# First-stage steps in other gaps and, for two batches, in whole passes, in a Fourier-mixing kernel with a fused feed-forward layer

## The chip, the cores and the metric

One core of one Trainium2 chip. The metric is the device time of one execution in microseconds (us), as the median of three runs. The engines are TensorE (PE, with its weight loads shown as PEld), VectorE (DVE), ScalarE (ACT), GpSimd (POOL) and SyncE (SP). ACT, POOL and SP also issue DMAs; each engine works through its own instructions in program order. All times below are us unless marked otherwise; in the profile's groups the mean of one instruction is in ns.

## What is computed

Eight batches of 3008 tokens with 256 channels are filtered in the frequency domain along the tokens, and the result goes through a feed-forward layer whose nonlinearity is h - tanh(h):

```python
X = np.fft.rfft(x, axis=1)                       # x: (8, 3008, 256)
Y = X * (filt_r + 1j * filt_i)[None]             # 1505 frequencies, 256 channels
y = np.fft.irfft(Y, n=3008, axis=1).reshape(-1, 256)
h = y @ w_in                                     # (24064, 256) @ (256, 2048)
out = (h - np.tanh(h)) @ w_out                   # (24064, 2048) @ (2048, 256)
```

## The kernel before, in words

**The stages.** The transform of 3008 = 64 x 47 points is done as matrix products. For one batch there are four stages:

- *first* (L245 to L280): the transform over the 64, for residues r and 47 - r at once. A step takes four residues: `x_sb` holds token rows of r in partitions 0 to 63 and those of 47 - r in 64 to 127, `f` the matrices. For each pair of PSUM banks it runs eight 64x64 products (quarters of the array); fp32 makes two passes of each, so the trace shows sixteen. ACT copies the second bank to `other` (L271), DVE writes sum and difference to `a1` (L272, L273), and two DMAs bring a1 to DRAM (`ct1`). Those are put on the list `written` and issued by ACT at the next gap (L1256). A batch has six such steps. Batch 0 and the first eight residues of batch 1 are done in a prologue instead, with whole 128-column passes (`first0`, `first1`).
- *middle* (L370 to L402): for seven slots of frequencies, products pa and pb (`forth`), the filter on DVE (`filtered`, L331 to L352), and the way back pe0 and pe1 (`back`, L362 to L367). It is a generator, with 58 steps that each issue one piece.
- *last* (L460): the product pu for 4 residues of tokens, ACT's copy `odd` (L475), DVE's sums into `ut` (L478, L479).
- the *feed-forward layer*: for each group of four residues (six groups c to a batch, 48 groups i) four units u, so U = 4i + u runs from 0 to 191. `up` (L499) multiplies by w_in into banks x, y, z (L512) with a Strassen-like scheme of seven products; ACT and DVE evacuate them (L518, L535, L552, L560, L568); `shrink` computes h - tanh(h) of the unit before with three ACT passes (L624, L627, L630) and a DVE product (L634); `down` multiplies the unit before that by w_out into o (L682). The first four units use the plain scheme (`up_plain`, L582, and `down_plain`, L736).

**The order.** It is written out by hand; the program order is each engine's order. In `up` five gaps t(0) to t(4) are left, in which other stages may issue. For batches 1 and up PE's order in a unit is

`x1 y2 | t(0) | o | t(1) | x6 z5 o | t(2) | x7 o x4 | t(3) | o | t(4) | z3`

Line L535, which reads bank y, is issued on DVE after t(0) and o. In t(k) (L1252) at most one planned step is issued, *last* always at u = 3, k = 2. The planner (`planned`) gives each step a due position on the scale pos = 20c + 5u + k; while batch p's tokens are computed it spreads six first-stage steps of batch p + 2 over 0.2 to 104, and the 58 middle steps of batch p + 1 likewise (for p = 0: ten first-stage steps, batch 1's last four and batch 2's six, from 4 to 34, and the middle steps from 34). A gap takes the first of the two next steps that is due and allowed.

**The banks.** Two PSUM banks, t and y, serve these stages. y is also unit U's own. A first-stage step and *last* take both (`zd2`), a middle product takes one (`zd`): y if a dictionary `taken`, kept by gap, says that t was given to another shortly before, else t. `taken` is cleared when a middle product comes in gap 0, and only then.

**The tiles.** `tr` has a1 with one buffer and e1 with two. Tag e1 is used for `other`, `odd`, the `e1` of `back`, and the a1 of `first1`'s last two steps (residues 4 to 7 of batch 1), whose stores SP issues (L1070).

**The end of the prologue** (L1126 to L1145). `rest` issues on SP the four loads of `e2` for slots 0 to 4 (L967), `way_back` then runs the last slot's `back`, whose stores go to ACT and SP (L367), and `rest` loads the other slots. Then come the first loads of `first(2, ...)` on SP (L253, L232, L238), the conversion of the float64 weights (`converted`: ACT L158, DVE L160, L163, L166, L169, L171, L178, one step at each `next`), first1's last stores and four steps of the remaining conversions. The conversions go on in the gaps of U = 0 to 5.

Of the kernel before, what the change touches and what calls it, by code (L numbers as in the profile page):

```python
# [9 lines left out]
F32 = mybir.dt.float32  # L10
# [15 lines left out]
XH = 4  # L26
# [22 lines left out]
def _consts():  # L49
    q = np.arange(NQ)[:, None]  # L50
    k1 = np.arange(1, NA)[None, :]

    def angle(r):
        return 2 * np.pi * ((k1 * (NR * q + r)) % SEQ) / SEQ

    def sign(r):
        return (-1.0) ** ((q[:, 0] + r) % 2)

    f = np.zeros((2, NQ, NH, 2, NA))
    g = np.zeros((4, NA, NH, 2, NQ))  # L60
    for r in range(NH):
        for half, n in ((0, r), (1, NR - r)):
            if half and not r:
                continue
            odd = 1.0 - 2 * half
            c, s = np.cos(angle(n)), np.sin(angle(n))
            plus, minus = (1 + sign(n)) / 2, (1 - sign(n)) / 2
            f[half, :, r, 0, :-1], f[half, :, r, 1, :-1] = c, -odd * s
            f[half, :, r, 0, -1], f[half, :, r, 1, -1] = plus, minus
            g[0, :-1, r, half], g[1, :-1, r, half] = 2 * c.T, -2 * s.T  # L70
            g[2, :-1, r, half], g[3, :-1, r, half] = -2 * odd * s.T, 2 * odd * c.T
            g[0, -1, r, half], g[2, -1, r, half] = plus, minus
            g[1, -1, r, half], g[3, -1, r, half] = odd * minus, odd * plus
    g = g[BLOCKS, :] / SEQ

    t = 2 * np.pi * (np.outer(np.arange(NH), np.arange(NH)) % NR) / NR
    cos, sin = np.cos(t), np.sin(t)
    twice = np.where(np.arange(NH) > 0, 2.0, 1.0)[:, None]
    mats = np.zeros((KM, 6 * KM + 8 * KH))
    for k, m in enumerate((cos, sin, -sin)):  # L80
        way = np.einsum("rm,st->srmt", m, np.eye(SG))
        mats[:, k * KM:k * KM + KM] = way.reshape(KM, KM)
        mats[:, (3 + k) * KM:(4 + k) * KM] = way.reshape(KM, KM).T
    for k, (a, b) in enumerate(((cos, cos), (cos, -sin), (sin, cos), (-sin, -sin),
                                (cos, twice * cos), (cos, -2 * sin),
                                (sin, twice * cos), (-sin, -2 * sin))):
# [5 lines left out]
    return [np.ascontiguousarray(v, dtype=np.float32)  # L92
            for v in (f.reshape(128, -1), g[:, :, :, 0].reshape(128, -1), g.reshape(128, -1),
                      mats, np.eye(128))]

@with_exitstack
def kernel(
# [8 lines left out]
):  # L106
    nc = tc.nc
    V, G, ACT = nc.vector, nc.gpsimd, nc.scalar
    f_d, g_d, whole_d, mats_d, one_d = (
        nc.inline_tensor(v, name=n).ap()  # L110
        for v, n in zip(_consts(), ("f", "g", "g_whole", "mats", "one")))

    ct1 = [nc.dram_tensor(f"ct1_{b}", (4 * NA * NH, DM), F32, kind="Internal")
           for b in range(1, BATCH)]
# [130 lines left out]
    def first(b, z, also=()):  # L245

        jobs = [*also, *((b, c) for c in range(NX))]

        def begin(k):
            b, c = jobs[k]  # L250
            w = XH * 64
            f = tr.tile([128, XH, 64], F32, tag="f", bufs=2, name="f")
            nc.sync.dma_start(f, f_d[:, w * c:w * (c + 1)])  # L253
            return load_x(tr.tile([128, XH, DM], F32, tag="x", bufs=2, name="x_sb"),
                          b, XH * c, XH), f

        began = [begin(0), begin(1)]
        yield
        for k, (b, c) in enumerate(jobs):
            xt, f = began.pop(0)  # L260
            banks = z("pf", [128, 2, DM])
            for n in range(2):
                for bank, half in zip(banks, rows):
                    for m, out_half in enumerate(rows):
                        nc.tensor.matmul(bank[out_half, n], f[half, 2 * m + n], xt[half, 2 * m + n],  # L265
                                         start=True, stop=True)
            if k + 2 < len(jobs):
                began.append(begin(k + 2))
            a1 = tr.tile([128, 2, 2, DM], F32, tag="a1", bufs=1, name="a1")
            other = tr.tile([128, 2, DM], F32, tag="e1", bufs=2, name="other")  # L270
            ACT.copy(other, banks[1])  # L271
            V.tensor_add(a1[:, 0], banks[0], other)  # L272
            V.tensor_sub(a1[:, 1], banks[0], other)  # L273
# [609 lines left out]
    with tc.tile_pool(name="tr", bufs=2) as tr, tc.manual_schedule():  # L883
# [12 lines left out]
        with tc.tile_pool(name="pro", bufs=1) as pro, \  # L896
# [163 lines left out]
            def first1(x1):  # L1060

                for r in range(0, 8, 2):
                    pf = z0("pf", [128, 2, DM])
                    for k in range(2):
                        nc.tensor.matmul(pf[:, k], f0[:, r + k], x1[:, r + k],
                                         start=True, stop=True)
                    a1 = (pro.tile([128, 2, DM], F32, tag="e1", bufs=4, name="a1") if r < 4 else
                          tr.tile([128, 2, DM], F32, tag="e1", bufs=2, name="a1"))
                    ACT.copy(a1, pf)
                    (ACT if r < 4 else nc.sync).dma_start(  # L1070
                        dram(ct1[1], r * DM, [[NH * DM, 128], [1, 2 * DM]]), a1)
                    yield
# [23 lines left out]
            for g in range(last_g + 1):  # L1096
                if g + 2 <= last_g:
                    fts[g + 2] = filters_of(g + 2)
                    a2[g + 2] = across(g + 2)
                if g == 3:  # L1100
                    e2s[0] = load_e2(0, 0, ())
                    ones_1 = first1(load_x(big([128, 8, DM], F32, "x1"), 1, 0, 8))
                if g == last_g - 1:
                    under(fts[last_g])
                    convert(3)
                    way_back()
                if g < last_g:
# [12 lines left out]
                if g not in (0, last_g - 1):  # L1120
                    way_back()
                if g == 1:
                    next(turning)
                if g == 2:
                    ahead = [begun(tiles1, job, queue=G) for job in jobs[5:7]]
            rest(0, SG * (last_g - 1), [nc.sync])  # L1126
            way_back()
            rest(SG * (last_g - 1), NA - SG * (last_g - 1), [nc.sync])
            fs = first(2, z2, [(1, c) for c in range(2, NX)])
            next(fs)  # L1130
# [3 lines left out]
            next(late)  # L1134
            for _ in ones_1:
                pass
            for _ in range(4):
                next(late)
            warmer(10)

        with tc.tile_pool(name="dn", bufs=2) as dn, \
# [4 lines left out]
            def zd(name, shape):  # L1146
                U, k = now
                if U < 4:
                    tag = taken["plain"] = "ty"[taken.get("plain") == "t"]
                    return ps.tile(shape, F32, tag=tag, bufs=1, name=name)  # L1150
                if k == 0:
                    taken.clear()
                tag = "y" if (k == 1 and taken.get(0) == "pb" or
                              k == 2 and taken.get(1) not in (None, "y") or
                              k == 3 and taken.get(2) != "y") else "t"
                taken[k] = "y" if tag == "y" else name
                return ps.tile(shape, F32, tag=tag, bufs=1, name=name)

            def zd2(name, shape):
# [47 lines left out]
            for U in range(total + 2):  # L1207
# [44 lines left out]
                def t(k):  # L1252

                    now[:] = U, k
                    while written:
                        ACT.dma_start(*written.pop(0))  # L1256
                    if k == 2 and stores:
# [77 lines left out]
```

## Time and profile before

| what | us |
|---|---|
| three runs | 2705.08, 2706.46, 2701.56 |
| median | 2705.08 |
| the profiled execution | 2712.48 |
| its span | 2710.6 |
| prologue, up to the first tokens' product in x (L582) | 0 to 96.5 |
| first-stage steps, first and last (L265) | 104.9, 1997.1 |

The profile is that of a single execution, which was itself a little longer than the runs. A row of the timeline gives the start in us from the span's start, the length, the engine, the line, the operation, out<-in, the count of merged instructions, and in brackets the idle time before it with what ended it. Matmuls overlap: a pass of 256 columns is shown at about 0.38, though the next one starts 0.216 behind it. A row of waits gives who waited for whom, the total, how often, and the longest. In the groups by line there follow busy time, mean of one in ns, and the idle time before, with its causes.

### The profile page before, as it was taken

The numbers are of one execution on the slowest core, as the hardware profiler recorded it, in microseconds if no ns is written. First come the engines' busy times: TensorE is split into PE (matmuls) and PEld (weight loads), VectorE is DVE, ScalarE is ACT, GpSimd is POOL, SyncE is SP. The second block draws the span as 40 slices with busy tenths as digits, with TensorE's granted clock in tenths as the row PEclk, the third lists the DMA queues.
The fourth block names the chain that finished last, engine by engine and source line by source line (L and its number), as shares of the span: only waits on it lengthen the run. The fifth ranks groups of instructions, "written<-read, shape, count | busy, mean of one in ns | idle before, by whom it ended". The sixth has DMA issues, their size and how long they took to land.

```text
span 2710.6 us, 41489 instructions
## 1 busy us (share of the span) xinstructions
PE 2644.6 (98%) x15540; PEld 2287.9 (84%) x15540; DVE 1805.7 (67%) x2254; ACT 1678.9 (62%) x2507; POOL 1303.8 (48%) x1084
## 2 busy tenths in 40 slices
PE   8889999999999999999999999999999999999998
PEld 6458888888898888988889888898888988898887
DVE  6787766676666666667656776577765776655555
ACT  3455666656666666666666666666666666666665
POOL 4115555454455444644445444455444554555552
PEclk9899999999999999999999999999999999999999
DMA  8754332331324313332234222332322222111110
GB/s 213 208 141 97 87 70 65 81 91 46 70 70 106 73 33 73 91 88 67 47 70 107 64 67 51 82 88 65 78 56 57 47 62 50 28 26 28 21 23 18
DMA packets 331881, 196.91 MB, mean 73 GB/s; under 512 B 225215, under 2 KB 302635, under 8 KB 331607
## 3 DMA queue, kind: packets, MB, share of 16 engines
q1 hardware_dynamic: 289357, 135.90, 21.6%
q10 hardware_dynamic: 38138, 45.63, 6.0%
q0 software_dynamic: 4176, 12.64, 1.7%
q8 instruction: 124, 2.03, 0.3%
q14 instruction: 86, 0.70, 0.1%
HBM read 121.91 MB, written 75.00 MB: 73 GB/s over the span
## 4 chain that ended last, share of the span: by engine, by line
PE 90%; DVE 5%; DMA 2%; issue 1%; ACT 1%; POOL 0%; SPq 0%; ACTq 0%; DVEq 0%; POOLq 0%
PE o L682 39%; PE x L512 23%; PE z L512 11%; PE y L512 5%; PE pe L362 3%; PE pu L471 2%; PE pa L314 2%; PE pf L265 1%; PE pb L314 1%; DVE h L634 1%; DVE xy L352 0%; DMA x<-in_x_dram 0%; DMA ct<-a 0%; DVE xy L351 0%; DMA mats_sb<-mats 0%
## 5 line engine op out<-in xcount | busy, mean ns | idle before, releaser
L682 PE MATMUL o<-t,wd 128*128 128x256 f32 (+1 forms) x3008 | 762.5, 376 | 0.0
L634 DVE TENSOR_TENSOR h<-h,y 128x1024 f32<-128x1024 f32 (+1 forms) x384 | 555.9, 1448 | 189.1 <-ACT y L630 188.6
L492 POOL TENSOR_TENSOR t<-h 128x512 f32<-128x512 f32 (+1 forms) x186 | 249.2, 1340 | 841.1 <-DVE h L634 782.2
L682 PEld LDWEIGHTS o<-t,wd 128*128 128x128 f32 x3008 | 572.0, 191 | 69.8 <-issue 3.9
L512 PE MATMUL x<-tu,wu 128*128 128x256 f32 (+1 forms) x2256 | 580.0, 380 | 4.4 <-ACT u L518 4.3
L682 PE MATMUL o<-h,wd 128*128 128x256 f32 (+1 forms) x2256 | 570.7, 376 | 1.8 <-DVE h L634 1.8
L512 PEld LDWEIGHTS x<-tu,wu 128*128 128x128 f32 x2256 | 421.3, 190 | 66.8 <-ACT u L518 10.5
L682 PEld LDWEIGHTS o<-h,wd 128*128 128x128 f32 x2256 | 428.7, 190 | 52.0 <-DVE h L634 2.6
L518 ACT COPY s<-x 128x512 f32<-128x512 f32 (+1 forms) x188 | 108.6, 578 | 532.9 <-PE x L512 527.1
L624 ACT ACTIVATE y<-h 128x1024 f32<-128x1024 f32 (+1 forms) x384 | 400.2, 1042 | 27.4 <-ACT e L365 8.0
L627 ACT ACTIVATE y<-y 128x1024 f32<-128x1024 f32 (+1 forms) x384 | 399.3, 1040 | 12.1
L630 ACT ACTIVATE y<-y 128x1024 f32<-128x1024 f32 (+1 forms) x384 | 399.9, 1041 | 4.7
L495 POOL TENSOR_TENSOR t<-h,t 128x512 f32<-128x512 f32 (+1 forms) x186 | 275.3, 1480 | 0.0
L518 ACT COPY u<-x 128x512 f32<-128x512 f32 (+1 forms) x376 | 214.6, 571 | 88.8 <-PE x L512 79.7
L493 POOL TENSOR_TENSOR t<-h,t 128x512 f32<-128x512 f32 (+1 forms) x186 | 261.0, 1403 | 14.6
L494 POOL TENSOR_TENSOR t<-h 128x512 f32<-128x512 f32 (+1 forms) x186 | 260.1, 1398 | 0.0
L560 DVE COPY h<-x 128x512 f32<-128x512 f32 (+1 forms) x188 | 127.8, 680 | 141.9 <-PE x L512 141.3
L512 PE MATMUL x<-ut,wu 128*128 128x256 f32 (+1 forms) x752 | 191.3, 377 | 4.1 <-DVE h L560 4.0
L512 PE MATMUL y<-ut,wu 128*128 128x256 f32 (+1 forms) x752 | 191.0, 377 | 0.0
L512 PE MATMUL z<-tu,wu 128*128 128x256 f32 (+1 forms) x752 | 191.0, 376 | 0.0
L552 DVE TENSOR_TENSOR h<-z,u 128x512 f32<-128x512 f32 (+1 forms) x188 | 126.7, 674 | 96.3 <-ACT u L518 95.0
L512 PE MATMUL z<-ut,wu 128*128 128x256 f32 (+1 forms) x752 | 190.8, 376 | 0.0
(160 smaller groups left out, 2965.3 us busy)
## 6 DMA issues: line engine op xcount, KB each, us to landing
e<-ct SPq DMA_DIRECT2D x47, 512.0 KB
ct<-a ACTq DMA_DIRECT2D x82, 256.0 KB
ct<-e ACTq DMA_DIRECT2D x86, 240.0 KB
a<-ct SPq DMA_DIRECT2D x42, 480.0 KB
ft<-filt SPq DMA_DIRECT2D x42, 480.0 KB
out_dram<-ot SPq DMA_DIRECT2D x1248, 16.0 KB
x_sb<-in_x_dram SPq DMA_DIRECT2D x74, 256.0 KB
gt<-g SPq DMA_DIRECT2D x48, 128.0 KB
```

The costliest lines, as they stand in the source:

```text
L492: by.tensor_sub(t[0], b[0][1], b[0][0])
L493: by.tensor_sub(t[1], b[1][1], t[0])
L494: by.tensor_sub(t[2], b[1][1], b[0][1])
L495: by.tensor_sub(t[3], b[1][0], t[1])
L512: nc.tensor.matmul(bank[:, k], wu[:, q - 1, (2 * u + k) * 128:(2 * u + k + 1) * 128], rhs[q - 1], start=(first and k == 0), stop=True, ski ...
L518: ACT.copy(t, X)
L560: V.tensor_copy(h[:, 2, :, 0:w], X)
L624: ACT.activation(y[k], ht[k], AF.Arctan, scale=TURN)
L627: ACT.activation(y[k], y[k], AF.Tanh, scale=BEND)
L630: ACT.activation(y[k], y[k], AF.Square, scale=SCALE, accum_out=y_sums[:, 2 * U + k // 2:2 * U + k // 2 + 1])
L634: V.tensor_mul(ht[k], ht[k], y[k])
L682: nc.tensor.matmul(product(q), wd[:, q - 1, (2 * u + k) * 128: (2 * u + k + 1) * 128], rhs[q - 1][:, k], start=(u == 0 and k == 0 and q == ...
```

## The change

1. `first` for batches up to 2 (ten steps): a matrix `f` of 128 columns from a new constant `both`, so that one whole pass gives both signs; four products (eight passes) in place of eight quarters, two ACT copies straight into a1, no `other` and no DVE sums, and one DMA from ACT right behind the copies. The tile `f` and its load grow from 128 to 256 KB for these steps.
2. `taken` is cleared at gap 0 of every unit from U = 4 on, and keeps the gap of the last "pb".
3. From U = 4 on a first-stage step may go only into gaps 1 and 2 of units 0 to 2, and not into the gap behind a "pb". Before, all gaps but 0 were allowed.
4. `first1`'s last two a1 are halves of one tile of tag a1, no longer e1.
5. `way_back` stands ahead of the first `rest`.
6. The four conversion steps at the prologue's end go; the same steps are then the first that come after the first tokens' *last*.

```diff
+    both = np.concatenate([f, np.stack([f[0], -f[1]])], axis=3)
...
         def begin(k):
             b, c = jobs[k]
-            w = XH * 64
-            f = tr.tile([128, XH, 64], F32, tag="f", bufs=2, name="f")
-            nc.sync.dma_start(f, f_d[:, w * c:w * (c + 1)])
+            n = 64 if b > 2 else 128
+            f = tr.tile([128, XH, 128], F32, tag="f", bufs=2, name="f")[:, :, 0:n]
+            w = XH * n
+            nc.sync.dma_start(f, (f_d if b > 2 else both_d)[:, w * c:w * (c + 1)])
...
             banks = z("pf", [128, 2, DM])
+            a1 = tr.tile([128, 2, 2, DM], F32, tag="a1", bufs=1, name="a1")
+            if b <= 2:
+                for m, bank in enumerate(banks):
+                    for n in range(2):
+                        nc.tensor.matmul(bank[:, n], f[:, 2 * m + n], xt[:, 2 * m + n],
+                                         start=True, stop=True)
+                    ACT.copy(a1[:, m], bank)
+                if k + 2 < len(jobs):
+                    began.append(begin(k + 2))
+                ACT.dma_start(dram(ct1[b], XH * c * DM, [[NH * DM, 128], [1, XH * DM]]),
+                              a1.rearrange("p m n c -> p (m n c)"))
+                yield
+                continue
...
-            a1 = tr.tile([128, 2, 2, DM], F32, tag="a1", bufs=1, name="a1")
...
+                    if r == 4:
+                        two = tr.tile([128, 2, 2, DM], F32, tag="a1", bufs=1, name="a1")
                     a1 = (pro.tile([128, 2, DM], F32, tag="e1", bufs=4, name="a1") if r < 4 else
-                          tr.tile([128, 2, DM], F32, tag="e1", bufs=2, name="a1"))
+                          two[:, r // 2 - 2])
...
+            way_back()
             rest(0, SG * (last_g - 1), [nc.sync])
-            way_back()
             rest(SG * (last_g - 1), NA - SG * (last_g - 1), [nc.sync])
...
-            for _ in range(4):
-                next(late)
             warmer(10)
...
-                if k == 0:
-                    taken.clear()
...
+                if name == "pb":
+                    taken["slow"] = k
...
                     now[:] = U, k
+                    if k == 0 and U >= 4:
+                        taken.clear()
...
                         due = [s for s in steps[0:2] if s[0] <= pos and
-                               (k or U < 4 or s[3] is middle)]
+                               (s[3] is middle or U < 4 or
+                                u < 3 and 0 < k < 3 and taken.get("slow") != k - 1)]
```

More of the change, by code (lines that the diff above doesn't have):

```diff
@@ L92, in _consts @@
     return [np.ascontiguousarray(v, dtype=np.float32)
-            for v in (f.reshape(128, -1), g[:, :, :, 0].reshape(128, -1), g.reshape(128, -1),
-                      mats, np.eye(128))]
+            for v in (f.reshape(128, -1), both.reshape(128, -1), g[:, :, :, 0].reshape(128, -1),
+                      g.reshape(128, -1), mats, np.eye(128))]
 @with_exitstack
@@ L108 @@
     V, G, ACT = nc.vector, nc.gpsimd, nc.scalar
-    f_d, g_d, whole_d, mats_d, one_d = (
+    f_d, both_d, g_d, whole_d, mats_d, one_d = (
         nc.inline_tensor(v, name=n).ap()
-        for v, n in zip(_consts(), ("f", "g", "g_whole", "mats", "one")))
+        for v, n in zip(_consts(), ("f", "f_both", "g", "g_whole", "mats", "one")))
     ct1 = [nc.dram_tensor(f"ct1_{b}", (4 * NA * NH, DM), F32, kind="Internal")
```

## The prediction, as it stood before the run

> **What bounds the kernel now.** I read the page's busy shares and its chain first, then the busy time by stretches, then PE's waits, and last the timeline at each wait.
>
> ```profile
> span 2710.6 us, 41489 instructions
> PE 2644.6 (98%) x15540; PEld 2287.9 (84%) x15540; DVE 1805.7 (67%) x2254; ACT 1678.9 (62%) x2507; POOL 1303.8 (48%) x1084
> PE 90%; DVE 5%; DMA 2%; issue 1%; ACT 1%; POOL 0%; SPq 0%; ACTq 0%; DVEq 0%; POOLq 0%
> ```
>
> PE is busy for nearly the whole span and holds 90% of the chain. The page's share is a mean over two different stages, so I asked for them apart (start and end, then busy time of PE, PEld, DVE, ACT, POOL, granted clock, DMA share, GB/s):
>
> ```profile
> 97.00:202.00 105.00, 94.88 (x470) 54.54 (x470) 88.30 (x161) 56.76 (x89) 11.93 (x13) 0.95 0.59 166
> 440.00:767.00 327.00, 323.14 (x1936) 282.35 (x1936) 220.06 (x267) 207.05 (x309) 163.38 (x132) 1.00 0.30 73
> ```
>
> From 97 to 202 us (units U = 0 to 6: batch 0's tokens while the weights are converted) PE is idle for a tenth and DVE, with conversions, is nearly as full. From 440 us on, each batch takes 327 us, and PE lacks only 3.9 of them. There PE is the limit: a pass more or a wait more costs its own length. So the waits decide (us in total, times, longest):
>
> ```profile
> PE pf L265 <- DVE xy L320: 7.6, 5, 1.5
> PE x L582 <- DVE ut L479: 6.2, 1, 6.2
> PE pe L362 <- DVE a L273: 5.4, 5, 1.1
> PE pa L314 <- issue: 5.2, 5, 1.0
> PE pe L362 <- DVE h L535: 1.2, 6, 0.2
> ```
>
> Four of the five come five times or six: once in each of the batches in which a batch's first stage (3 to 7) runs beside the tokens. The 6.2 is the start of the first tokens.
>
> **The change, part by part.**
>
> *The gaps of the quarter steps.* I worked through the planner's list: due times of a first-stage step 17.3 apart, those of the 58 middle steps 1.79 apart, one step to a gap, the gap of the tokens' own first product left out. As (token group c, unit u, gap k), the six steps of each of batches 3 to 7 lie now at (0,0,1), (0,3,4), (1,3,1), (2,2,3), (3,2,1), (4,1,3). By the new rule they lie at (0,0,1), (1,0,1), (2,0,1), (3,0,1), (3,2,2), (4,2,1).
>
> What goes: at (3,2,1) a step takes both banks one gap after "pb" took t; and after (2,2,3) and (4,1,3) a middle product wants t one gap behind. The timelines of PE and DVE show the first, a step without a wait (535.05), and one of the latter (start, length, instruction):
>
> ```profile
> 535.05 1.10 PE L265 MATMUL pf<-x_sb,f 64*64 64x256 f32 x16
> 536.08 1.13 PE L512 MATMUL x<-tu,wu 128*128 128x256 f32 x4
> ...
> 633.33 1.67 PE L682 MATMUL o<-h,wd 128*128 128x256 f32 x7
> 636.53 1.59 PE L265 MATMUL pf<-x_sb,f 64*64 64x256 f32 x16 [1.53 <-DVE xy L320]
> 638.05 1.13 PE L512 MATMUL x<-tu,wu 128*128 128x256 f32 x4
> ...
> 686.44 1.13 PE L682 MATMUL o<-t,wd 128*128 128x256 f32 x4
> 688.65 1.09 PE L362 MATMUL pe<-xy,mats_sb 120*120 120x256 f32 x4 [1.08 <-DVE a L273]
> ```
>
> and the chain gives the spacing of whole passes, eight in 1.73, 0.216 each:
>
> ```profile
> 207.93 1.73 PE o L682 x8
> ```
>
> A step without a wait holds PE for 536.08 - 535.05 = 1.03. At (3,2,1) seven passes from 633.33 end at 634.84, and X goes on at 638.05: 3.21, of which 1.03 is the step and some 0.1 the change of shape, so 2.1 is waiting. After (4,1,3), four passes from 686.44 end at 687.30 and pe starts at 688.65: 1.35. The wait of pa after (2,2,3) is as long by the waits (5.2 beside 5.4 for five): 1.3. In group 5, pe waits for L535 because a stale record put it into bank y; the record is now cleared at each unit's gap 0, so it goes to t: 0.2 to 0.4, say 0.3. Together 2.1 + 1.35 + 1.3 + 0.3 = 5.05 a batch, **25.2 for five**.
>
> What comes: the rule knows of "pb", but not of a late read of bank y, which L535 does on DVE. At (1,0,1), (3,0,1) and (4,2,1) the gap before holds a pe, a pe and a product on SBUF, with L535 in time; (3,2,2) comes two gaps after pb. At (2,0,1), however, gap 0 gives DVE L351 and L352 ahead of L535. That unit before, where no first-stage step follows:
>
> ```profile
> 546.11 1.03 PE L512 MATMUL z<-ut,wu 128*128 128x256 f32 x4
> 548.70 1.89 PE L682 MATMUL o<-h,wd 128*128 128x256 f32 x8
> 550.43 1.03 PE L512 MATMUL x<-tu,wu 128*128 128x256 f32 x4
> ...
> 545.80 1.21 DVE L349 TENSOR_TENSOR nn<-nn,xy 120x512 f32<-120x512 f32 x1
> 546.93 1.21 DVE L634 TENSOR_TENSOR h<-h,y 128x1024 f32<-128x1024 f32 x1
> 548.07 0.68 DVE L568 TENSOR_TENSOR h<-z,u 128x512 f32<-128x512 f32 x1
> 548.67 1.45 DVE L351 TENSOR_TENSOR xy<-nn 120x512 f32<-120x512 f32 x1
> 550.04 1.76 DVE L352 TENSOR_TENSOR xy<-nn 120x512 f32<-120x512 f32 x1
> 551.73 0.68 DVE L535 TENSOR_TENSOR h<-y,s 128x512 f32<-128x512 f32 x1
> ```
>
> The step would start at 550.43 and want y after its first four quarter passes, at about 550.85. L535 ends at 552.41: a wait of 1.55. But L349 moves two gaps earlier with its "sub", and L272/L273 of the old (1,3,1) leave the unit before, so L568 need not wait for L634: z's passes from 546.11 are done about 547.1, up to 0.9 earlier than 548.07. So the wait is 0.7 to 1.55; I take 1.1, **5.5 for five**. Queued behind it on PE is everything (X's passes, the next o products), so it counts in full. Net of the gaps: **-19.7** (bounds -17.5 and -21.7 by that wait).
>
> *Whole passes for batches 1 and 2* (ten steps, U = 0 to 6; only U = 5's second moves, to U = 6's gap 2). PE: eight passes of 0.216 = 1.73 for 1.03 and two changes of shape of some 0.1, so +0.5 to +0.7 a step, **+6**. The Trainium skill (TensorEngine Tiling (Array Packing), Available Configurations) has four independent 64x64 tiles; by it sixteen quarter passes would last as long as four whole ones, 0.86, and the edit would cost 0.87 a step, 8.7 in all. The rows have the quarters dearer than that, and they decide.
>
> What DVE and ACT lose and get (busy us, mean ns, idle time before):
>
> ```profile
> L272 DVE TENSOR_TENSOR a<-pf,other 128x512 f32<-128x512 f32 x10 | 6.9, 688 | 7.5 <-DMA ct<-a 4.1 <-ACT other L271 2.7 <-ACT conv L158 0.6
> L273 DVE TENSOR_TENSOR a<-pf,other 128x512 f32<-128x512 f32 x10 | 6.8, 680 | 0.0
> L160 DVE TENSOR_SCALAR conv<-conv 128x512 f32<-128x512 f32 x10 | 4.6, 465 | 4.4 <-ACT conv L158 4.4
> L163 DVE TENSOR_SCALAR conv<-conv 128x512 int32<-128x512 int32 x10 | 4.5, 453 | 0.3
> L166 DVE SCALAR_TENSOR_TENSOR conv<-raw,conv 128x512 int32<-128x512 int32 x10 | 6.9, 690 | 0.3
> L271 ACT COPY other<-pf 128x512 f32<-128x512 f32 x10 | 5.8, 579 | 7.5 <-PE pf L265 7.5
> L1256 ACTq DMA_DIRECT2D ct<-a x20: 582/619/686, 108.0 to 195.9; - x20
> ```
>
> DVE loses 13.7 of adds, and its 7.5 of waits ahead of them pass to ACT. ACT gets a second copy (+5.8) and loses ten of twenty DMA issues (-6.2): even. SP loads f with 256 instead of 128 KB, ten times. The four conversion steps taken out of the prologue are ACT's scaling and L160, L163, L166: 0.47 + 0.45 + 0.69 = 1.6 of DVE work that lay in idle time and now falls behind the first tokens' sums. The new hold: a1 has one buffer, so ACT's copy of the next step waits for the last one's DMA, with the activations, the h and u copies and the conversions' scaling queued behind it; hardest at U = 6, gaps 1 and 2, some 5 apart. Ends for the stage: all of DVE's relief counts, -13.7 - 4.1 + 1.6 = -16; none of it counts, +6. PE, 94.88 of 105 busy, has 10 to give and takes 6 more, so the middle of what is left, **-6**.
>
> *The first tokens.* ACT, SP and PE at their start:
>
> ```profile
> 87.98 2.40 PE L471 MATMUL pu<-gt,e 64*64 64x64 f32 x64 [3.60 <-DMA e<-ct]
> 96.55 3.36 PE L582 MATMUL x<-ut,wu 128*128 128x448 f32 x4 [6.17 <-DVE ut L479]
> 94.72 0.58 ACT L475 COPY odd<-pu 128x512 f32<-128x512 f32 x1 [8.51 <-DMA ct<-a]
> 89.57 1.02 SPq L1070 DMA_DIRECT2D ct<-a  x2
> ```
>
> pu is done at 90.4, but its copy "odd" starts at 94.72: its e1 buffer is that of first1's third a1, whose store SP issues only at 89.57, behind the loads. With a1 in a buffer of its own, odd can start at about 90.5: **-4.2**. Late next is nothing but pu, and pu waits for e<-ct. way_back before rest puts two stores ahead of four loads on SP; the last loads wait for those stores either way: 0, at most +1.5 if the four land later.
>
> **Sum**: -19.7 - 6 - 4.2 = -29.9. The profiled execution took 2712.48 (its span and 1.9 around it), so it would take 2682.6; it lies 7.4 above the median of the runs, 2705.08, and off that the forecast is **2675.2**.
>
> **Rivals.**
>
> 1. *The wait on y is longer and comes at more gaps.* For it: L351 and L352 above take 1.45 and 1.76, and L349, of the same 120x512, took 1.21; a DVE that falls behind by one such excess at (1,0,1), (3,0,1) and (2,0,1) makes waits of about 0.5, 0.5 and 2. The batches then save 25.2 - 15 = 10: 2685. Against it: pe, not a DVE sum, stands in gap 0 of two of them. The Trainium skill (GPSIMD Engine Reference, Specifications) has POOL share SBUF interfaces with DVE, in contention with instructions of two SBUF inputs; L351 and L352 are such, and POOL's combination would start earlier there, so by it the wait grows rather than shrinks; the rows of 1.21 and 1.76 agree.
> 2. *The early stage gives nothing:* PE's +6 is paid and DVE's relief ends in waits for the raw weights or for a1. -19.7 - 4.2 + 6 = -17.9: 2687. For it: the DMA share of 0.59 and ACT's 4.4 ahead of L160.
> 3. *L535 is always in time and DVE was the early limit:* -25.2 - 4.2 - 12 = -41: 2664.
> 4. *Slower: ACT held by a1's single buffer.* With the hold h at each of the ten early steps passed on to PE, 6 + 10h stands against 23.9 saved; it decides from h = 1.8 on. At the 4.1 of the one such wait above it is 6 + 41 - 23.9 = +23: 2728. Against it: of ten such waits nine didn't occur, with steps mostly 5 to 15 apart.
> 5. *The rule doesn't reach what it means:* the steps meet as long a wait in the new gaps (25 against 25), and the early stage pays what the start saves: 2705.
>
> **How the numbers follow.** Forecast 0.50 (2666 to 2684), rival 1 0.17, rival 2 0.15, rival 3 0.12, rival 4 0.04, rival 5 0.02. The range takes in the forecast and rivals 1 and 2 with some 4 for the runs' own spread, and the half of rival 3 that lies nearer: 2663 to 2691. A measurement of this kernel tells about 0.2%, 5.4 us. All but rivals 4 and 5 are faster by more: 0.94; the same 0.02; slower 0.04.
>
> **What would show it.** Right: no wait of pf on L320, none of pe on L273 or pa; a wait of pf on L535, five times about 1; a batch of about 323.4 in place of 327.3; "odd" right behind pu, U = 0 at about 92.4; L272 and L273 thirty times instead of forty; U = 7 some 10 earlier than at 202. Wrong: ACT's copies of a1 waiting for ct<-a for several us in U = 1 to 6, PE's x waiting for ACT there, or a batch still at 327.

## The result, and the profile after

| | before | after |
|---|---|---|
| median | 2705.50 | 2680.40 |
| runs | 2701.56 to 2706.46 (4) | 2680.11 to 2681.72 (4) |
| span of the profiled execution | 2710.6 | 2678.3 |

The ratio is 0.9911, with a 95% interval of 0.9894 to 0.9928: 25.1 us faster, beside 29.9 forecast. The medians put the time at 2680.4, 5.2 above the point of the forecast and inside its range. The two profiles differ by 32.3, since the profiled execution of before lay above its median. One execution of before in a later series of runs took 2794.03 at a granted clock of 0.945 and is left out of the medians and ratios below.

In the changed kernel the lines have moved: the quarters' product L265 is now L280 and the adds L272 and L273 are L286 and L287; the whole passes have L268, their copies to a1 L270 and their DMA L273; L312 to L402 and what follows stand 14 further down (L512 is L526, L535 is L549, L362 is L376, L475 is L489, L582 is L596, L736 is L750). The head of the page after:

```profile
span 2678.3 us, 41269 instructions
PE 2641.6 (99%) x15460; PEld 2292.6 (86%) x15460; DVE 1780.1 (66%) x2234; ACT 1684.2 (63%) x2517; POOL 1312.4 (49%) x1084
PE 91%; DMA 3%; DVE 2%; issue 1%; ACT 1%; SPq 1%; POOL 0%; ACTq 0%; DVEq 0%; POOLq 0%
```

PE has 80 instructions fewer and nearly the same busy time, 2641.6 for 2644.6: the gain is idle time, not work. The busy time by stretches of after, for U = 0 to 6 and for one later batch (columns as before):

```profile
92.00:193.00 101.00, 97.76 (x391) 64.82 (x392) 78.41 (x145) 62.95 (x100) 12.14 (x13) 0.95 0.63 193
428.00:752.00 324.00, 322.64 (x1935) 281.98 (x1935) 218.88 (x267) 207.02 (x309) 163.43 (x132) 1.00 0.31 74
```

In the batch PE now lacks 1.4 of 324 where it lacked 3.9 of 327. In the early stretch PE lacks 3.2 of 101 (it lacked 10.1 of 105), with DVE's load 10 lower and ACT's 6 higher. PE's waits after, over the whole span (some rows left out):

```profile
PE pu L485 <- DMA x_sb<-in_x_dram: 4.9, 1, 4.9
PE x L526 <- ACT u L532: 4.6, 6, 0.9
PE o L750 <- DVE wd L179: 3.2, 1, 3.2
PE x L596 <- DVE ut L493: 1.9, 1, 1.9
PE pf L280 <- DVE h L549: 1.4, 5, 0.5
```

The three waits that came five times in before (7.6 of pf for xy, 5.4 of pe, 5.2 of pa) are gone. Three stand in their place: five of pf for L549, as forecast; x for ACT's u, five of them in the later batches (before has 4.3 of these in four waits, all ahead of the batches); and a single one of 3.2 for the weights. The last two the forecast did not have. The lengths of stretches, read from the timelines (start of the first x product of a unit to that of the next; each batch's 24 units from U = 24):

| | before | after |
|---|---|---|
| start of U = 0 | 96.5 | 91.9 |
| U = 0 to 6 | 105.2 | 100.5 |
| of these, U = 2 | 18.3 | 15.5 |
| of these, U = 3 | 17.9 | 23.2 |
| of these, U = 4 | 18.4 | 14.3 |
| of these, U = 5 and 6 | 34.0 | 30.3 |
| U = 7 to 23 | 238.8 | 234.9 |
| of these, U = 9 | 18.1 | 14.1 |
| five batches with first-stage steps | 327.3 327.3 327.3 329.0 327.6 | 324.4 324.1 324.5 324.3 324.1 |
| the batch without them | 315.3 | 314.8 |

### The profile page after: what moved, and what is told of

The parts are those of the page before. It is cut to its first block, busy times and chain, and to the rows that moved or that the text cites. A ratio compares the mean times of both kernels' runs of the same rounds, so it can differ in the third digit from the quotient of the medians.

```text
span 2678.3 us, 41269 instructions
## 1 busy us (share of the span) xinstructions
PE 2641.6 (99%) x15460; PEld 2292.6 (86%) x15460; DVE 1780.1 (66%) x2234; ACT 1684.2 (63%) x2517; POOL 1312.4 (49%) x1084
## 3 DMA queue, kind: packets, MB, share of 16 engines
q8 instruction: 123, 2.02, 0.3%
## 4 chain that ended last, share of the span: by engine, by line
PE 91%; DMA 3%; DVE 2%; issue 1%; ACT 1%; SPq 1%; POOL 0%; ACTq 0%; DVEq 0%; POOLq 0%
PE o L696 40%; PE x L526 24%; PE z L526 12%; PE y L526 6%; PE pe L376 3%; PE pu L485 2%; PE pb L328 2%; PE pa L328 1%; PE pf L280 1%; PE o L750 1%; DMA out_dram<-ot 1%; DMA filt<-in_filt_r_dram 1%; SPq L802 0%; PE pf L268 0%; DMA ct<-a 0%
## 5 line engine op out<-in xcount | busy, mean ns | idle before, releaser
L506 POOL TENSOR_TENSOR t<-h 128x512 f32<-128x512 f32 (+1 forms) x186 | 256.4, 1379 | 819.2 <-DVE h L648 763.6
L526 PE MATMUL x<-tu,wu 128*128 128x256 f32 (+1 forms) x2256 | 580.5, 380 | 4.7 <-ACT u L532 4.6
L526 PEld LDWEIGHTS x<-tu,wu 128*128 128x128 f32 x2256 | 418.7, 190 | 73.8 <-issue 12.5
L532 ACT COPY u<-x 128x512 f32<-128x512 f32 (+1 forms) x376 | 215.1, 572 | 100.5 <-PE x L526 76.6
L507 POOL TENSOR_TENSOR t<-h,t 128x512 f32<-128x512 f32 (+1 forms) x186 | 266.6, 1433 | 14.6
L509 POOL TENSOR_TENSOR t<-h,t 128x512 f32<-128x512 f32 (+1 forms) x186 | 264.3, 1421 | 0.0
L508 POOL TENSOR_TENSOR t<-h 128x512 f32<-128x512 f32 (+1 forms) x186 | 261.0, 1403 | 0.0
L526 PE MATMUL x<-ut,wu 128*128 128x256 f32 (+1 forms) x752 | 190.3, 375 | 0.0
L526 PE MATMUL y<-ut,wu 128*128 128x256 f32 (+1 forms) x752 | 190.1, 375 | 0.0
L526 PE MATMUL z<-tu,wu 128*128 128x256 f32 (+1 forms) x752 | 190.0, 375 | 0.0
L526 PE MATMUL z<-ut,wu 128*128 128x256 f32 (+1 forms) x752 | 190.0, 375 | 0.0
```

Of the source, the lines that this page charges most:

```text
L506: by.tensor_sub(t[0], b[0][1], b[0][0])
L507: by.tensor_sub(t[1], b[1][1], t[0])
L508: by.tensor_sub(t[2], b[1][1], b[0][1])
L509: by.tensor_sub(t[3], b[1][0], t[1])
L526: nc.tensor.matmul(bank[:, k], wu[:, q - 1, (2 * u + k) * 128:(2 * u + k + 1) * 128], rhs[q - 1], start=(first and k == 0), stop=True, ski ...
L532: ACT.copy(t, X)
```

## The experiments

My theory was that of the forecast: the batches' gain comes from the gaps (parts 2 and 3 of the change) and is cut by a wait on y in one unit; the early gain comes from DVE's relief, and is cut by something in U = 3. The rivals were that the whole passes or the free banks alone make it, that ACT, held by a1's single buffer, is what costs U = 3, and that the steps taken out of the prologue are. Each kernel was timed in five rounds beside before; the changed kernel ran again as the control.

> The changed kernel itself, as the base for the others of this call. Theory and rival alike: within 0.2% of 0.9911 times the kernel before, that is 2684.8 us where the kernel before takes 2708.9.

It took 2682.35 (2678.25 to 2684.68), ratio 0.9905 [0.989, 0.9919]. The medians of before in the three series of runs were 2708.87 (x1 to x4), 2707.9 (the control, x6, x7, x9) and 2707.63 (x10, x11, x8, x5), so kernels of different series are compared by their ratios.

### The gaps: taken back, and alone

x1_old_gaps is the changed kernel with the old rule and the old clearing:

```diff
+                if k == 0:
+                    taken.clear()
...
-                if name == "pb":
-                    taken["slow"] = k
...
-                    if k == 0 and U >= 4:
-                        taken.clear()
...
-                               (s[3] is middle or U < 4 or
-                                u < 3 and 0 < k < 3 and taken.get("slow") != k - 1)]
+                               (k or U < 4 or s[3] is middle)]
```

> The changed kernel with the old rule for gaps and the old clearing of the bank record (whole passes up to batch 2 and first1's own buffer stay). Theory, that five batches gained by the gaps: the waits of pf on the reads after pb (5 x 1.5 us shown idle), of pe on the DVE sums and of pa come back, a batch takes 327.3 us again in place of 324.2, and the time is 2680.4 + 17.6 = 2698 us (2695 to 2701). Rival, that the gain sits in the early stage and the batches only look shorter by the clock: 2680 to 2685 us.

2699.91 (2698.78 to 2703.68), ratio 0.9969 [0.9957, 0.9981]. Its waits of PE from 427 us on:

```profile
PE pf L280 <- DVE xy L334: 7.6, 5, 1.5
PE pe L376 <- DVE a L287: 5.4, 5, 1.1
PE pa L328 <- issue: 5.2, 5, 1.0
PE pe L376 <- DVE h L549: 1.3, 6, 0.2
```

The rows of before, to a tenth, and four of its five batches are 327.3 again, the fifth 328.9. Its unit 9 is 18.9, too.

x10_gaps_alone is the kernel before with just these lines of the change put in (the diff above, read backwards).

> The kernel before with the new rule for gaps and the new clearing of the bank record, nothing else. Theory, that the gaps' gain is independent of the early stage: batches of 324.3 us in place of 327.3 (17.6 us), and unit 9, which took 18.1 us before and 18.9 with the old gaps in the changed kernel, back to 14.2 to 15 (3 to 4 us more): 0.992 to 0.9935 times the kernel before, 2688 to 2692 us where that takes 2709. Rival, that unit 9's length comes from the early stage: 0.9935 to 0.995.

2686.66 (2685.71 to 2688.51), ratio 0.9924 [0.9911, 0.9938]: 21.0 of the change's 25 to 26 come from the gaps alone. Four of its five batches took 323.6 to 324.3, one 325.9. Two things went otherwise than I had worked out. Unit 9 fell only from 18.1 to 17.1, not to the 14 of the changed kernel. And U = 5 and 6 fell from 34.0 to 29.4, though nothing but one first-stage step left U = 5. DVE's waits in the early stage, first of before, then of x10:

```profile
DVE conv L160 <- ACT conv L158: 4.4, 3, 2.8
DVE a L272 <- DMA ct<-a: 4.1, 1, 4.1
DVE a L272 <- ACT other L271: 2.7, 3, 1.2
```

```profile
DVE conv L160 <- ACT conv L158: 4.6, 3, 2.9
DVE a L272 <- ACT y L630: 2.4, 1, 2.4
DVE a L272 <- ACT other L271: 2.3, 3, 1.2
```

The wait of 4.1 for a store of a1 is gone in x10: with two first-stage steps close together in U = 5, the second add found a1 still being stored. The new gaps put them apart. So part of what the forecast counted as DVE's relief by whole passes is had by the gaps alone.

### The wait on y at (2,0,1)

The timelines of after at U = 32, DVE's row first and then PE's (the rows of both, by start):

```profile
536.55 0.68 DVE L549 TENSOR_TENSOR h<-y,s 128x512 f32<-128x512 f32 x1
537.29 1.08 PE L280 MATMUL pf<-x_sb,f 64*64 64x256 f32 x12 [0.48 <-DVE h L549]
538.30 1.13 PE L526 MATMUL x<-tu,wu 128*128 128x256 f32 x4
```

Four of the sixteen quarter passes went before L549 had read y, the other twelve behind it. The idle time shown is 0.48, but passes in flight are shown longer than they hold PE, so the cost of the wait is better read from the unit's length in x6. x6_late_read tells the rule of the step that sends DVE two xy sums ahead of L549, as if it were a "pb":

```diff
             if before:
                 next(before[0])
+                taken["slow"] = now[1]
                 yield
```

> The changed kernel, in which a gap behind the middle stage's last sums (L365, L366 of the changed kernel, which keep DVE from reading bank y) is barred to a first-stage step too; the step of (2,0,1) goes to (2,0,2). Theory, that the wait of pf on DVE h L549 (0.5 us shown idle in the view, 1.2 us a batch by unit 32's length) is that late read: unit 32 of each batch is 1.1 us shorter, the batches 323.2 in place of 324.3, 5.5 us in all. Rival, that the wait moves with the step (pb then asks for a bank one gap later): no change.

2677.61 (2676.01 to 2678.77), ratio 0.9892 [0.9876, 0.9908]. PE's waits of x6 from 427 us on (its lines stand one further down):

```profile
PE x L527 <- ACT u L533: 4.8, 6, 0.9
PE x L527 <- ACT s L533: 1.3, 1, 1.3
```

No wait of pf is left. U = 32 took 14.2 in every batch of x6, and in after 15.29 in the first of the five and 15.02 to 15.07 in the others: the wait was 1.1 once and 0.85 to 0.9 four times, 4.6 in all, beside the 4.7 between the control and x6. So the wait that the forecast priced from L535's row at 1.1, with bounds of 0.7 and 1.55, is 0.9 in the mean. L365 and L366 ahead of it took 1.53 and 1.75, as their forerunners did in before (1.45 and 1.76): the contention with POOL that the Trainium skill (GPSIMD Engine Reference, Specifications) describes may be in these lengths already, but the earlier start did not add to it.

### What remains in the batches: unit 42

By the forecast's terms the batch should be 323.4, and is 324.3. U = 42 is 15.32 long in after and 12.95 in before. One first-stage step has come to it; the same made U = 36 longer by 1.22 (13.82 to 15.04). The other 1.15 is a wait. ACT's wait in after, 430 to 2300 us:

```profile
ACT u L532 <- DMA out_dram<-ot: 11.1, 5, 2.3
```

and the timeline there, PE, ACT, DVE and SP together:

```profile
680.15 1.30 DVE L775 STREAM_TRANSPOSE ot<-o 128x512 f32<-128x512 f32 x2
680.56 1.03 PE L376 MATMUL pe<-xy,mats_sb 120*120 120x256 f32 x4
680.88 9.19 SPq L802 DMA_DIRECT2D out_dram<-ot  x18
681.62 0.59 ACT L379 COPY e<-pe 120x512 f32<-120x512 f32 x1 [0.82 <-PE pe L376]
684.03 0.35 ACTq L381 DMA_DIRECT2D ct<-e  x1
684.42 0.59 ACT L532 COPY u<-x 128x512 f32<-128x512 f32 x1 [2.21 <-DMA out_dram<-ot]
685.06 1.13 PE L526 MATMUL x<-tu,wu 128*128 128x256 f32 x4 [0.88 <-ACT u L532]
```

ACT has its tile e at 682.2, but its store of e goes out at 684.03 and the copy u right behind it, and PE's x waits for u. What ended ACT's idle time was the landing of an output store that SP had issued, which neither e nor u reads or writes. So the store ct<-e was held until that landing. In before no u in the batches had such a wait. Unit 9 had one in before, though, and has it in x1 (the old gaps, above), where unit 9 takes 18.9:

```profile
226.55 0.37 ACTq L381 DMA_DIRECT2D ct<-e  x1
226.96 1.06 ACT L638 ACTIVATE y<-h 128x1024 f32<-128x1024 f32 x1 [3.69 <-DMA out_dram<-ot]
```

Again ACT's store of e goes out late, and what stands behind it waits 3.69 for an output store.

If the store were held because the output stores are issued too early in the gap, issuing them last should release it. x9_stores_last does that, on top of x6's edit and of x4's (below):

```diff
                         store(*stores.pop())
-                    store_some(4)
                     if U >= total:
+                        store_some(4)
                         return
...
                             next(gens[b])
+                    store_some(4)
                     converting(2)
```

> The last kernel, with SP's out stores issued behind a gap's step instead of ahead of it. Theory, that in unit 42 ACT's store of pe1 waits because it counts on the semaphore of an out store issued just ahead of it in the same gap (11.1 us of ACT's waits, 5 times; 1.0 us of PE a batch): that wait goes, 5 us less than the last kernel. Rival, that the stores run late by DVE's transposes and any of them hits ACT at another gap: within 2 us of the last kernel, either way.

2671.19 (2669.27 to 2671.68), ratio 0.9865 [0.9849, 0.9881], beside 2673.6 and 0.9875 [0.9859, 0.9891] for x7, the same without this edit. Of the 2.5 between their two profiles 1.3 are in the five batches together (the fifth alone is 324.9 and 323.2 long), and 1.0 in the start of U = 0; U = 42 is 15.3 in both. What makes these isn't settled. The wait did not move:

```profile
ACT u L535 <- DMA out_dram<-ot: 11.1, 5, 2.3
```

So that idea fell: the place of the output stores within the gap isn't it. The trace shows the wait and what ends it; why ACT's store waits for an output store of SP's stays open, and no run shows that the two share a semaphore, as the expectation has it. One run is without the wait, x5 below: there ACT issues one store for the first-stage step in this unit, where after has two (L1272, at 679.80). Whether that is the reason wasn't tried.

### Whole passes: none, and everywhere

x3_quarters is the change with quarters for batches 1 and 2 as well:

```diff
-            n = 64 if b > 2 else 128
+            n = 64
...
-            nc.sync.dma_start(f, (f_d if b > 2 else both_d)[:, w * c:w * (c + 1)])
+            nc.sync.dma_start(f, f_d[:, w * c:w * (c + 1)])
...
-            if b <= 2:
+            if b < 0:
```

> The changed kernel with quarters, DVE sums and two stores for batches 1 and 2 too. Theory, that DVE's 13.7 us of sums outweigh PE's 6 us more: units 0 to 6 take about 105 in place of 100.9 us and the time is 2684.5 us (2682.5 to 2690; the upper end if the steps in gaps 1 and 2 of unit 6 now hold DVE for a store). Rival, that the whole passes cost what they bring: 2679 to 2681.5 us, and if PE's passes were the limit there, 2675 us.

2687.81 (2685.67 to 2692.55), ratio 0.9925 [0.9912, 0.9939]. U = 0 to 6 took 104.0, beside 100.5 and 100.3 in after and the control. The whole passes are worth 3.5 by these lengths and 5.4 by the ratios (0.9925 beside 0.9905, intervals that just overlap), although they cost PE more. Unit 9 has a part in it: 17.0 in x3, 14.1 and 14.8 in after and the control.

x5_whole_all takes whole passes for all batches (n = 128, `both_d`, and `if b <= 7`). Here the price of a whole step is measured directly.

> The changed kernel with whole passes for all batches (forty steps in place of ten), so that the price of a whole step is read where PE is the limit. Theory: eight passes of 0.216 us for 1.03 and two changes of shape of 0.1, +0.6 us a step, less some 0.6 a batch where the step now wants bank y later: 324.3 + 3.1 = 327.4 us a batch, 2682 + 15.5 = 2698 us (2694 to 2702). Rival, by the rule of four independent 64x64 tiles (0.86 us a quarter step): +0.87 a step, 5 a batch, 2707. Rival, that freeing DVE of its sums pays it back: 2685 or less.

2685.8 (2684.36 to 2686.37), ratio 0.9917 [0.9904, 0.9931]: 3 above the control by the ratio, with intervals that overlap, far less than I expected. The first step of a batch in x5, and the same one in the control:

```profile
429.86 1.89 PE L268 MATMUL pf<-x_sb,f 128*128 128x256 f32 x8
431.59 0.92 PE L526 MATMUL x<-tu,wu 128*128 128x224 f32 x4
```

```profile
429.39 1.09 PE L280 MATMUL pf<-x_sb,f 64*64 64x256 f32 x16
430.42 1.02 PE L526 MATMUL x<-tu,wu 128*128 128x224 f32 x4
```

A whole step holds PE for 1.73, a quarter step for 1.03 and about 0.1 at each side where the shape changes (the x product behind it is shown 0.10 longer, too). The difference by the units' lengths is 0.50 (14.80 for 14.30 in U = 24, 15.55 for 15.04 in U = 36 and 38). The Trainium skill (TensorEngine Tiling (Array Packing), Available Configurations) has four independent 64x64 tiles. With four quarters always beside one another the difference would be 0.87, by the forecast's estimate; the measured 0.50 decides against that. Yet a batch of x5 is longer by only 1.1 (325.4 for 324.3), since part of the six steps' +3.0 is given back: U = 42 is 14.68 for 15.32, which is before's 12.95 and a step of 1.73 with no wait at all, and U = 32 is 14.87 in each batch (15.29 in the first batch of after, 15.02 to 15.07 in the others).

### a1's buffer, and the steps taken out of the prologue

Unit 3 of after takes 23.2 where before took 17.9. The rows of PE in after:

```profile
126.11 0.91 PE L750 MATMUL o<-h,wd 128*128 128x448 f32 x2
130.24 1.86 PE L750 MATMUL o<-h,wd 128*128 128x448 f32 x2 [3.21 <-DVE wd L179]
131.89 3.19 PE L596 MATMUL z<-ut,wu 128*128 128x448 f32 x4
134.88 2.56 PE L268 MATMUL pf<-x_sb,f 128*128 128x256 f32 x8
```

PE waits 3.2 for a converted weight (L179 is the last step of a conversion), and the next o then takes 1.86 for 0.91: PE is slower after the wait, not only late. Two causes offered themselves. ACT's copies to a1 wait for the store of the step before (ACT's waits, 84 to 193 us):

```profile
ACT a L270 <- DMA ct<-a: 3.0, 2, 2.8
```

with the stores landing as late as the chain of after shows (start, length of the transfer):

```profile
102.21 7.13 DMA ct<-a
110.52 5.12 DMA ct<-a
```

The second lands at 115.64, and ACT's next copy to a1 starts at 115.71. The other cause: the four conversion steps that the prologue no longer does.

x4_two_a1 gives the even steps of batches 1 and 2 a second buffer (a tile that is free then), and leaves the prologue as changed:

```diff
-            a1 = tr.tile([128, 2, 2, DM], F32, tag="a1", bufs=1, name="a1")
+            a1 = (tr.tile([128, 4, DM], F32, tag="nn", bufs=1, name="a1").rearrange(
+                      "p (m n) c -> p m n c", n=2) if b <= 2 and k % 2 == 0 else
+                  tr.tile([128, 2, 2, DM], F32, tag="a1", bufs=1, name="a1"))
```

> The changed kernel with a second buffer for a1 in the ten whole steps (every other one uses the tile nn, which is free until unit 7). Theory, that ACT held by the landing of a1's store costs time in units 1 to 3: ACT's waits on ct<-a (3.0 us, 2 times) go, with what queues behind them, and the time is 2677 us (2674 to 2679). Rival, that the early units wait for the raw weights and DVE's conversions anyway: 2680 to 2681 us.

2676.74 (2675.49 to 2678.25), ratio 0.9881 [0.9866, 0.9896]. That is 6.5 below the control by the ratio. ACT's wait on ct<-a is gone, and U = 3 takes 17.1.

x8_order_back leaves a1 with one buffer and takes back parts 5 and 6 of the change:

```diff
-            way_back()
             rest(0, SG * (last_g - 1), [nc.sync])
+            way_back()
...
+            for _ in range(4):
+                next(late)
```

> The changed kernel with rest ahead of way_back and with the four conversion steps in the prologue, as before. Theory, that the order on SP is worth nothing and the four steps lie in idle time there: DVE has 1.6 us less to do behind the first tokens' sums, and the time is 0 to 2 us under the changed kernel (0.9895 to 0.9911 of the kernel before). Rival, that way_back's second store, which waited 4 us for a free semaphore behind rest's loads, holds the last loads again: pu starts 1 to 3 us later and so does the end.

2676.89 (2675.43 to 2678.11), ratio 0.9885 [0.987, 0.99]: 5.4 below the control by the ratio, where I had expected up to 2. U = 3 takes 17.0, although ACT's hold is there as in after:

```profile
ACT a L270 <- DMA ct<-a: 4.2, 2, 3.7
```

So in the kernels with whole passes neither cause is enough alone: with the hold and without the four steps done ahead, the weight is late; x4 and x8 each take one of the two away, and it is in time. (x8 takes back part 5, the order on SP, as well; the two parts were not separated. Nor is it shown that a semaphore was what the store in its expectation waited for.) x3 says that the hold isn't the only partner. It has neither whole passes nor the four steps, and PE waits for the same weight:

```profile
110.59 1.21 PE L280 MATMUL pf<-x_sb,f 64*64 64x256 f32 x16 [2.02 <-issue]
111.73 2.99 PE L750 MATMUL o<-h,wd 128*128 128x448 f32 x4
130.80 1.02 PE L750 MATMUL o<-h,wd 128*128 128x448 f32 x2 [3.11 <-DVE wd L179]
```

There DVE has its sums back; what holds the conversion in x3 was not looked for by a run of its own. PE between 125 and 138 us in after, x8 and x4:

```profile
125.00:138.00 13.00, 9.79 (x22) 5.32 (x21) 9.75 (x20) 5.41 (x9) 1.45 (x2) 0.74 0.52 149
```

```profile
125.00:138.00 13.00, 13.00 (x99) 7.51 (x99) 12.26 (x26) 9.65 (x16) 0.58 (x1) 1.00 0.73 233
```

```profile
125.00:138.00 13.00, 12.96 (x99) 7.25 (x98) 9.64 (x20) 9.32 (x15) 0.72 (x1) 1.00 0.85 268
```

The granted clock (third figure from the end) is 0.74 over these 13 us, in the other two 1.00. So the wait of 3.2 costs 6 in U = 3 (4.8 in the control, whose U = 3 is 21.8). The length of a wait doesn't say by itself whether this happens: in x3 the clock over the same 13 us is 1.00 and the two passes behind the wait of 3.11 took 1.02, while the four behind the wait of 2.02 took 2.99, with a clock of 0.74 from 110.5 to 117.

x7_late_two has x4's and x6's edits together.

> The last kernel's rule and a second buffer for a1 in the ten whole steps together. Theory, that the two are separate places (units 1 to 3, and unit 32 of each batch): 5.5 + 6 = 11.5 us under the changed kernel of this call. Rival, that the waits of ACT's stores for a free completion count of an out store shift with every change: anything from 0 to 12.

2673.6 (2672.74 to 2673.98), ratio 0.9875 [0.9859, 0.9891]: U = 3 is 17.1, and there is no wait of pf. x9, which is x7 with the output stores last, is the best version run: 11.2 below the control by the medians of their series. x7 or x9 together with x8's edit was not tried.

### The first tokens

x2_e1_back puts first1's last two a1 back to tag e1.

```diff
-                    if r == 4:
-                        two = tr.tile([128, 2, 2, DM], F32, tag="a1", bufs=1, name="a1")
...
-                          two[:, r // 2 - 2])
+                          tr.tile([128, 2, DM], F32, tag="e1", bufs=2, name="a1"))
```

> The changed kernel with first1's last two tiles again under tag e1 (all else stays). Theory, that odd's buffer was what held the first tokens: odd waits again for the store that SP issues behind the loads, the product in x starts about 4.2 to 4.7 us later, near 96.5, and the time is 2685 us (2683 to 2686.5). Rival, that the order of way_back on SP or the four conversion steps did it: 2680 to 2681 us, x at 92.

2686.93 (2683.88 to 2687.84), ratio 0.9916 [0.9903, 0.993], beside the control's 0.9905 [0.989, 0.9919]: intervals that overlap. In its profile odd is held for 12.05 until ct<-a, and U = 0 starts at 95.0. x11_buffer_alone is the kernel before with only part 4 of the change (the same diff, read backwards).

> The kernel before with first1's last two tiles under tag a1, nothing else (rest ahead of way_back, the four conversion steps in the prologue). Theory, that the buffer alone starts the first tokens earlier: x at 92 in place of 96.5, and the conversions no later: 4 to 6 us less than the kernel before, 0.998 to 0.9985. Rival, that odd then waits for a store of way_back's on SP behind rest's loads: x at 94 or later and less than 2.5 us.

2705.5 (2700.14 to 2706.92), ratio 0.9987 [0.9978, 0.9997]: 2.1 from medians to the series' before, where I had expected 4 to 6; the interval of the ratio is 0.8 to 6.0. Its timeline:

```profile
87.67 0.59 ACT L475 COPY odd<-pu 128x512 f32<-128x512 f32 x1 [4.32 <-issue]
89.50 3.35 PE L582 MATMUL x<-ut,wu 128*128 128x448 f32 x4 [1.91 <-DVE ut L479]
```

There U = 0 starts 7.0 ahead of before's 96.5; in after it is 4.6 ahead:

```profile
87.49 2.49 PE L485 MATMUL pu<-gt,e 64*64 64x64 f32 x64 [4.91 <-DMA x_sb<-in_x_dram]
90.06 0.59 ACT L489 COPY odd<-pu 128x512 f32<-128x512 f32 x1 [8.99 <-issue]
91.89 3.35 PE L596 MATMUL x<-ut,wu 128*128 128x448 f32 x4 [1.91 <-DVE ut L493]
```

odd is right behind pu in both, as forecast. But in the profiles of the kernels with the new buffer U = 0 starts anywhere from 89.5 to 91.9, and of those with the old one at 93.8 (x10), 95.0 (x2) and 96.5 (before), so a single pair says little of 4 us there. The medians say 2 to 3, with intervals that hold 4 as well.

## Why the forecast was right, and where it was not

**The gaps.** Right in mechanism, order and most of the size. A step without a wait makes its unit 1.22 longer (U = 27 and 31, which lost one, U = 36, which got one). With that taken off, U = 34, 38, 41 and 44 are shorter by 1.28, 2.09, 1.32 and 0.44: 5.1 a batch beside 5.05 forecast, term by term (1.3, 2.1, 1.35, 0.3). The wait of pf on L549 came five times, at 0.9 for the 1.1 taken (U = 32 is 2.34 longer in the first batch and 2.06 to 2.11 in the others, 1.22 of it the step). **The step that failed** is the sentence that at (4,2,1) a step has "L535 in time" and so costs only itself. On y it was; but with the step in that gap a store of ACT's meets the landing of an output store, and 1.15 a batch are lost by ACT's u. I looked at what the new gap does to bank y, and not at what the shift by one step does to ACT's queue, where a DMA's issue stands ahead of u. So a typical batch gave 3.0, 15 in all, in place of 19.7. In the profiles it is 17.1, because before's had a batch of 329.0.

**Unit 9.** Not in the sum at all: 18.1 to 14.1 in after, so 3 to 4. It is the same kind of wait as U = 42's, in reverse: here the change happened to remove one. It takes two parts of the change together: 17.1 with the gaps alone (x10), 17.0 without the whole passes (x3), 18.9 without the gaps (x1).

**Early stage, -6.** About right as a sum (100.5 for 105.2, so -4.7), which is luck, for it was wrong in its parts. Already -6 is more than the forecast's own PE row leaves, 10.1 of idle time less 6 for the added passes. "Only U = 5's second moves" counted as nothing on its own, but it takes DVE's wait of 4.1 with it and is worth 4.6 in U = 5 and 6 (x10). The whole passes give 2.8 in U = 2 and 4.1 in U = 4 (15.5 and 14.3 in after, 18.4 and 19.4 in x3, 18.3 and 18.4 in x10); in U = 2 what went is a wait of pf of 2.0 and the slower passes behind it, which before, x3, x10 and x11 have and no kernel with whole passes has. The mis-sized term is the four conversion steps, priced at 1.6 of DVE's time: in U = 3 they cost 5 to 6, because together with the hold on a1 they put a weight's conversion behind PE's need for it, and the slower clock nearly doubled the damage. Without that U = 0 to 6 take 94.8 (x8, from 89.5 to 184.3), 10 less than before. PE is busy for 94.6 of them, at a granted clock of 0.98 for 0.95 in before, so its busy time in before was no lower bound. The price of a whole step, +0.5 to +0.7, is measured at 0.50.

**First tokens, -4.2.** The mechanism is right, as is the row (odd directly behind pu). As a size it is 4.6 by the profiles of before and after, and 2 to 3 by medians (x11, x2), whose intervals are too wide to decide between 2 and 4.2.

**Rivals.** Rival 4 (ACT held by a1) was real but of about two holds, 3.0 in all, and mattered only with the four steps gone; it took some 5 to 6 and not 41. Rival 1's longer waits on y didn't come at (1,0,1) and (3,0,1). Rival 3's 12 in the early stage is near x8's 10, though no run shows that DVE was the limit there; its L535 always in time didn't come. Rivals 2 and 5 fell: the early stage gives 4.7, and x1's rows are those of before.

**The sum.** The change is worth 25.1 by the first runs and 25.6 by the control's: batches 15, U = 0 to 6 about 4.7, first tokens 2 to 3, unit 9 3 to 4. From the start of the last unit to the end the profile of after is 1.5 shorter, but the kernels with the change take anything from 36.2 to 38.0 there, and before 37.9, so nothing is counted for that. The forecast's point was 5.2 too low, 0.4 of it because before's median is now 2705.50. The batches fell short by 4.7, and it is luck that what the parts left out or mis-sized (unit 9, U = 2 to 5, the first tokens) about cancels.

## What to carry to other kernels

When a planned step moves to another gap, follow every instruction queued behind it on every engine, the DMA issues too: here the bank waits came out as worked out, and a store's wait on ACT, which no bank explains, took a fifth of the gain back. An edit that defers work from an idle stretch is priced at what it makes late, not at its own length, and two harmless delays on the way to one weight can be harmful together. Where the bound engine falls idle for some us, look at its clock behind the wait.

## What the runs showed of the hardware that I had not expected

- After a wait of 3.2 us on PE two passes of 448 columns took 1.86 instead of 0.91, and the granted clock over 13 us was 0.74: the wait of 3.2 lengthened its unit by 6. In x3 a wait of 3.11 at the same place left the clock at 1.00, and one of 2.02 was followed by 0.74 over 6.5 us.
- Whole 128-column steps of eight passes cost only 0.50 more than sixteen quarter passes (1.73 against 1.03 and about 0.1 at each change of shape).
- A store of 512 KB that ACT issues (ct<-a) landed 5.1 and 7.1 us after its issue in the early stage (chain of after), where a landing sets when ACT may go on.
- An ACT store issued 1.8 us late behind the landing of SP's output store, with 1.15 a batch on PE; its cause in the trace stays open.
